# Chunk states by a scan that reads the sums in PSUM, and longer groups of small products on TensorE

## Chip, cores and metric

The kernel runs on one core of one Trainium2 chip. The metric is the device time of one execution in microseconds (us). TensorE (PE) multiplies matrices into PSUM, VectorE (DVE), ScalarE (ACT) and GpSimd (POOL) do the elementwise work, and SyncE (SP) issues every DMA, all on one queue.

## What is computed

Three stages run one after the other over 4 batches of 768 tokens: a gated linear attention with 8 heads of 48, a mixing block with a squared ReLU and a sigmoid gate, and a low-rank token mixing with a two-layer ReLU network.

```python
for t in range(S):                                   # attention, S = 768, D = 48
    state = alpha[:, :, t, :, None] * state + einsum('bhd,bhe->bhde', k[:, :, t], v[:, :, t])
    y[:, :, t] = einsum('bhd,bhde->bhe', q[:, :, t], state)
...
xk = mu_k * x + (1 - mu_k) * x_prev                  # first block; xr likewise with mu_r
k = maximum(xk @ w_k, 0);  v = k * k @ w_v;  r = sigmoid(xr @ w_r);  x = r * v
...
u = x + (x.T @ U @ V).T                              # second block
out = u + maximum(u @ w_ch1, 0) @ w_ch2
```

## The kernel before

**Tiling.** The tokens are cut into 8 half batches ("blocks") of 384 tokens. A block has two attention *units* of four heads, and a unit has two *phases* (`ph`) of two heads, one on partitions 0 to 47 (`EV`), the other on 64 to 111 (`OD`). There are 16 units. Even blocks are the first half of a batch, odd blocks the second; `unit(u)` gives that as `half`. A block's tokens are three chunks of 128 (`NC`, `CH`).

**Attention of a unit.** `prep` (line 700) makes, for each phase, running products of alpha with two DVE scans (`G` backwards, `Fp` forwards), the chunk factors `fc`, the scaled keys `KB` and the scaled queries `QG`. `scores` (722) multiplies keys by queries: three chunks for each of two heads, six products of 48x128 by 48x128, the heads in banks 6 and 7, then a DVE mask into `SC`. `keys_by_token` (733) transposes the three chunks of keys on PE into bank 5 and copies them (`KI`). `states` (742) makes the sums of keys times values, 12 small products (48 columns) in bank 5, and from them the states at the chunks' starts: ACT spreads the factors (`FX`) and copies the sums out of PSUM (`KV`, line 754), in a second half the carried state is scaled by ACT (four pieces) and added by DVE (two), DVE scans (multiply, then add), and two DVE products with the factors write the states `ST`. `outputs` (770) adds values times scores and states times queries, products with 128 columns in banks 6 and 7, and ACT copies the result into `x`; six small DMAs then spread a quarter of its rows over three tiles.

**Dense part.** `moe1` (897) and `moe2` (991) are long runs of products with 384 columns, three for each float32 pair (high and low parts). All eight blocks of `moe1`, with the attention of the following blocks woven in, come before all of `moe2`.

**Order.** Nothing is ordered by hand. `Plan` records every operation with a price in ns and a due time; `schedule` (186) lists them engine by engine, 11 times over with priorities drawn from the last pass, and keeps the order with the earliest planned end. On PE a switch between large products and small ones (`SHORT`: scores 165, outputs 107, states 60) has a price, so after a small product the next small one that is ready goes first if its priority is within `BATCH` of the best large one (line 242). Where the plan sees PE idle it puts a *fill* product (tile `warm`, line 395) of 56 ns, which writes nothing that is read. `dma` (361) prices a load by its words.

**Storage.** Keys, queries and alphas of a phase go to one of three tiles `T`. Converted rows of the second block's result leave through `x2_ring`, two slots; a third row tile waits until the DMA of the first has left its slot. Each fp32 product counts as two records in the trace; the large ones are fp32r and count as one.

Of the kernel before, what the change touches and what calls it, by code (L numbers as in the profile page):

```python
# [19 lines left out]
P = 128  # L20
# [23 lines left out]
    mix0_k=468, wk0=-238, wk1=-283, wk2=-17, wk3=45, wk4=60, wkk=7, wv=-12, r0=5, wr=37, early=31, x2=25, u=48, w1=227,  # L44
# [8 lines left out]
BATCH = 3000.0  # L53
# [26 lines left out]
class Plan:  # L80
# [265 lines left out]
    def scan(self, out, d0, d1):  # L346
        self.add(
            "DVE", 66.0 + 2.085 * out.free_size(), [out], [d0, d1],
            lambda: self.nc.vector.tensor_tensor_scan(  # L349
                out=out, data0=d0, data1=d1, initial=0.0, op0=ALU.mult, op1=ALU.add  # L350
            ), True,
        )
# [7 lines left out]
    def dma(self, out, in_, out_key=None, in_key=None, cost=650.0):  # L360
        words = 1
        for d in out.shape:
            words *= d
        self.add(
            "SP", max(cost, words / 90.0), [out if out_key is None else out_key], [in_ if in_key is None else in_key],
# [36 lines left out]
def fast_path(nc, plan, arena, rounded, shared, banks, qka, v, mus, w_k, w_r, w_v, U, V, w_1, w_2, out, x2d, ok_i):  # L402
# [45 lines left out]
    fc = new(NPH, NC)  # L448
# [10 lines left out]
    raw_at = [words(arena, 2 * TB) for _ in range(4)]  # L459
    raw_n = [0]  # L460
# [30 lines left out]
    FX, R = (att(2, D, NC) for _ in range(2))  # L491
    ST = [att(2, 2, NC, D) for _ in range(2)]
    KV = new(2, D, NC)
    carry = new(2, 2, D)
    G, Fp, bt = (att(TB) for _ in range(3))
    aC = new(NC)
# [57 lines left out]
    plan.dve(400, [bt], [], lambda: nc.vector.memset(bt, 0.0))  # L554

# [12 lines left out]
    plan.pool(130, [FX[:, :, :, 0]], [], lambda: nc.gpsimd.memset(FX[:, :, :, 0], 0.0))  # L568
    for t in banks[5:8]:
        plan.dve(600, [t[32:64]], [], lambda t=t: nc.vector.memset(t[32:64], 0.0))  # L570
# [104 lines left out]
    def tile_of(ph):  # L675
        return T[{2: 0, 3: 1, 0: 2, 1: 0}[ph] if ph < 4 else ph % 3]

    def load_qka(ph, parts=((0, KD),), rows=D, to=None):
# [4 lines left out]
        for a, z in parts:  # L683
            for hh in range(2):
                src = qka[b, h0 + hh, half, 0, a, 0]
                plan.dma(
                    t[64 * hh : 64 * hh + rows, a * TB : z * TB],
                    bass.AP(src.tensor, src.offset, [[KD * TB, rows], [1, (z - a) * TB]]), in_key="in", cost=475.0,
# [7 lines left out]
    def check_pair(ph, t):  # L696
        there = junk[:, 0 : t.free_size()].rearrange("p (c t) -> p c t", c=t.shape[1])
        plan.act(there, t, AF.Relu, scale=-1.0, bias=ALPHA_MIN, accum_out=low[:, ph : ph + 1])

    def prep(ph, due, engs):  # L700

        qt, kt, at = q_k_a(tile_of(ph))
        g0, f, a0 = G[:, 0:TB:CH], fc[:, ph, :], firsts[:, ph, :]
# [4 lines left out]
        first = at[:, 0:TB:CH]  # L708
        plan.act(a0, first, AF.Copy)
        plan.act(first, ends[:, 0:NC], AF.Copy)  # L710
# [3 lines left out]
        plan.pool(163, [f], [a0, g0], lambda: nc.gpsimd.tensor_tensor(out=f, in0=a0, in1=g0, op=ALU.mult))  # L714
        plan.at = due + 6
        plan.scan(Fp, at[:, 0:TB], bt)
        plan.at = due + 14
        plan.tt(KB[ph % 2], kt, G, ALU.mult, engs[0])
        plan.at = due + 17
        plan.tt(QG[ph % 4], qt, Fp, ALU.mult, engs[1])  # L720
# [13 lines left out]
    def keys_by_token(ph, due):  # L734
        plan.at = due
        kt, kb = sub(kk_b, NC, 112), KB[ph % 2]
        for c in range(NC):
            plan.transpose(kt[:, c, :], kb[BOTH, c * CH : (c + 1) * CH], ident[BOTH, BOTH])
        for h, r in enumerate((EV, OD)):
            plan.act(KI[ph % 2][:, h], kt[:, :, r], AF.Copy)  # L740
# [653 lines left out]
```

## Time and profile before

| | us |
|---|---|
| median of 3 runs | 724.15 (722.25 to 725.62) |
| the profiled execution, its own time | 724.62 |
| its span, first to last instruction | 722.9 |
| PE busy | 705.5 (98%) |
| DVE busy | 508.5 (70%) |
| ACT busy | 354.5 (49%) |
| fill products on PE | 581 |

The span has three parts. Up to about 127 us (the start) the attention of the first blocks is made, weights are loaded and converted, and large products begin; fill products stand there up to 73 us. From 127 to 450 us `moe1` runs with attention woven in. From 450 us on there are only `moe2` and its conversions. In a timeline row the length of merged products reaches to the modelled end of the last one, which overlaps the next row; how long a group holds PE is read from its start to the start of the next row.

### The profile page before, as it was taken

The page shows a single profiled execution, that of the slowest core. Times are in us where ns is not written, and L with a number is a line of the kernel's source. Part 1 is how long each engine was busy: PE and PEld are TensorE (multiplying, and loading weights), DVE is VectorE, ACT ScalarE, POOL GpSimd, SP SyncE. Part 2 cuts the span into 40 slices and gives each one's busy share as a digit, 9 for nine tenths or more (in the row PEclk, how much of TensorE's full clock was granted, in tenths as well). Part 3 has the DMA queues.
Part 4 walks back from the last instruction along what each step waited for, and adds up shares of the span by engine and source line. Part 5 has one row for each costly group of instructions (what it writes and reads, how often), then busy time and mean ns, then how long its engine had stood idle before and what let it go on. Part 6 is the DMA issues. An engine that isn't in the chain of part 4 may idle for free.

```text
span 722.9 us, 13907 instructions
## 1 busy us (share of the span) xinstructions
PE 705.5 (98%) x5319; PEld 675.4 (93%) x5319; DVE 508.5 (70%) x1173; ACT 354.5 (49%) x901; POOL 75.8 (10%) x131
## 2 busy tenths in 40 slices
PE   7999999999999999999999999999999999999995
PEld 7798889899999999999999999999999999999995
DVE  6898987897776567773699999575665657474611
ACT  2588656976767557677797672212121112111210
POOL 2021101442130311311002100000000000000000
PEclk9999989999999999999999999999999999999998
DMA  8835733434333222313253240102020202020001
GB/s 222 200 102 157 186 84 102 108 94 109 85 98 75 63 62 60 98 51 99 65 153 110 66 143 16 51 0 66 1 67 1 65 1 67 1 66 2 34 1 37
DMA packets 29484, 55.46 MB, mean 77 GB/s; under 512 B 5344, under 2 KB 20064, under 8 KB 29408
## 3 DMA queue, kind: packets, MB, share of 16 engines
q1 hardware_dynamic: 29408, 54.48, 27.3%
q8 instruction: 43, 0.70, 0.4%
q14 instruction: 33, 0.27, 0.1%
HBM read 43.85 MB, written 9.44 MB: 74 GB/s over the span
## 4 chain that ended last, share of the span: by engine, by line
PE 74%; DVE 6%; ACT 4%; DMA 3%; issue 1%; SPq 1%; DVEq 0%; ACTq 0%
PE bank L305 73%; DMA arena<-in_qka_dram 3%; ACT arena L320 2%; DVE arena L137 2%; DVE arena L982 2%; DVE rounded L137 1%; PE bank L310 1%; SPq L366 1%; ACT rounded L320 1%; DVE shared L137 1%; ACT shared L320 1%; DMA out_dram<-arena 0%; ACT bank L320 0%; DVE shared L349 0%; DVEq L137 0%
## 5 line engine op out<-in xcount | busy, mean ns | idle before, releaser
L305 PE MATMUL bank<-rounded 128*128 128x384 f32 x2232 | 424.3, 339 | 2.9 <-ACT rounded L320 1.2
L305 PEld LDWEIGHTS bank<-rounded 128*128 128x128 f32 x2232 | 383.7, 186 | 13.2 <-ACT arena L320 2.2
L305 PE MATMUL bank<-rounded,shared 128*128 128x384 f32 x864 | 164.9, 335 | 0.8 <-DVE rounded L137 0.5
L320 ACT ACTIVATE rounded<-bank 128x384 fp32r<-128x384 f32 x160 | 78.3, 489 | 175.4 <-PE bank L305 174.3
L305 PEld LDWEIGHTS bank<-rounded,shared 128*128 128x128 f32 x864 | 150.9, 188 | 1.7 <-DVE rounded L137 1.0
L320 ACT ACTIVATE arena<-arena 128x384 f32<-128x384 f32 (+6 forms) x234 | 103.2, 463 | 48.2 <-DMA arena<-in_qka_dram 29.4
L137 DVE SCALAR_TENSOR_TENSOR rounded<-bank,rounded 128x384 fp32r<-128x384 f32 x96 | 53.4, 556 | 91.4 <-ACT rounded L320 90.3
L982 DVE STREAM_TRANSPOSE arena<-arena 32x96 f32<-32x96 f32 x384 | 103.8, 270 | 5.7
L305 PE MATMUL bank<-shared 128*48 128x128 f32 (+3 forms) x1472 | 100.3, 266 | 3.4 <-DMA shared<-in_v_dram 1.2
L305 PEld LDWEIGHTS bank<-shared 128*48 128x48 f32 (+2 forms) x1472 | 86.6, 142 | 17.8 <-issue 6.2
L320 ACT ACTIVATE rounded<-arena 128x384 fp32r<-128x384 f32 (+2 forms) x137 | 70.4, 522 | 63.6 <-DVE arena L982 49.4
L137 DVE SCALAR_TENSOR_TENSOR arena<-arena 128x384 int32<-128x384 int32 (+2 forms) x140 | 79.9, 590 | 8.9 <-ACT arena L320 8.3
L320 ACT ACTIVATE bank<-bank 128x384 f32<-128x384 f32 x128 | 61.6, 482 | 23.4 <-PE bank L305 22.7
L137 DVE TENSOR_TENSOR rounded<-arena,rounded 128x384 fp32r<-128x384 f32 (+1 forms) x108 | 60.5, 570 | 11.4 <-ACT rounded L320 10.9
L137 DVE TENSOR_TENSOR arena<-bank,arena 128x384 f32<-128x384 f32 (+1 forms) x76 | 41.5, 552 | 25.0 <-PE bank L305 9.9
L137 DVE TENSOR_TENSOR rounded<-bank,rounded 128x384 fp32r<-128x384 f32 x64 | 35.4, 552 | 30.6 <-ACT rounded L320 28.9
L320 ACT ACTIVATE arena<-bank 112x384 f32<-112x384 f32 (+3 forms) x76 | 37.3, 504 | 35.2 <-PE bank L305 33.3
L137 DVE TENSOR_TENSOR shared<-bank,arena 128x384 f32<-128x384 f32 x64 | 33.9, 547 | 24.5 <-PE bank L305 23.0
L137 POOL TENSOR_TENSOR rounded<-arena,rounded 128x384 fp32r<-128x384 f32 (+1 forms) x25 | 27.7, 1116 | 110.5 <-ACT rounded L320 110.4
L395 PE MATMUL bank<-warm 128*128 128x128 bf16 x581 | 37.4, 224 | 1.1 <-DVE arena L543 1.1
L395 PEld LDWEIGHTS <-warm 128*128 128x128 bf16 x581 | 34.5, 101 | 3.1 <-issue 1.5
L349 DVE TENSOR_TENSOR_SCAN shared<-arena 128x384 f32<-128x384 f32 x32 | 31.0, 967 | 4.4 <-ACT arena L320 4.3
(47 smaller groups left out, 258.3 us busy)
## 6 DMA issues: line engine op xcount, KB each, us to landing
arena<-in_qka_dram SPq DMA_DIRECT2D x56, 216.0 KB, 3.7
arena<-in_w_dram SPq DMA_DIRECT2D x24, 384.0 KB, 3.5
shared<-in_v_dram SPq DMA_DIRECT2D x32, 144.0 KB, 3.0
x2d<-arena SPq DMA_DIRECT2D x24, 192.0 KB, 2.2
arena<-x2d SPq DMA_DIRECT2D x8, 576.0 KB, 4.1
out_dram<-arena SPq DMA_DIRECT2D x24, 192.0 KB, 1.9
arena<-in_w_v_dram SPq DMA_DIRECT2D x8, 384.0 KB, 3.2
arena<-in_qka_dram SPq DMA_DIRECT2D x24, 72.0 KB, 2.0
```

What stands on the lines that cost most here:

```text
L137: fn(**args)
L305: "PE", cost, [out], [lhsT, rhs], lambda out, lhsT, rhs: fn(out, lhsT=lhsT, rhs=rhs, start=start, stop=stop),
L310: self.add("PE", cost, [out], [in_, ident], lambda: self.nc.tensor.transpose(out, in_, ident))
L320: self.add("ACT", cost, outs, [in_] + extra, lambda out, in_: fn(out, in_, func, **kw), out=out, in_=in_)
L349: lambda: self.nc.vector.tensor_tensor_scan(out=out, data0=d0, data1=d1, initial=0.0, op0=ALU.mult, op1=ALU.add), True,
L366: lambda: self.nc.sync.dma_start(out, in_),
L395: lambda i: nc.tensor.matmul(banks[SPARE[i]][:, 384:512], lhsT=warm, rhs=warm, start=True, stop=True), FILL_UNTIL, ROUNDS
L982: plan.dve(284, [to], [src], lambda to=to, src=src: nc.vector.transpose(out=to, in_=src))
```

## The change

- `states`: the products write each sum with a stride of four words into bank 5 (one slot more than before, `NC + 1`). The scan reads the sums straight from PSUM, adds first and then multiplies by the factor, so that its results are the states; ACT copies them into `ST`. The DVE products, the ACT copy of the sums and, in a second half, the scaling and adding of the carried state are gone: the carried state is copied by ACT into the spare slot of bank 5. In a second half the last chunk's state is not needed, and its keys are not transposed and its sums not made.
- `prep`: the lower bound on the decay is taken inside the scan `G` (its second operation is a maximum), in place of a POOL operation ahead of the reciprocal.
- Planner: `BATCH` 3000 to 15000, a load is priced at words/56 in place of words/90, and the due times of the `w_k` loads are others; their pieces are 1, 1, 3, 1, 1, 1 in place of 1, 2, 3, 1, 1 columns of 128.
- A fourth tile `T[3]` lies over two buffers of weights, so that all four phases of the first block have their own tile. In the first block the spreading DMAs follow the unit that is made first.
- `moe2`: the three result tiles go to `rs`, three slots, in place of `x2_ring`.
- Several operations take 112 partitions in place of 128.

```diff
-    mix0_k=468, wk0=-238, wk1=-283, wk2=-17, wk3=45, wk4=60, wkk=7, ...
+    mix0_k=468, wk0=-238, wk1=-230, wk2=-220, wk3=38, wk4=45, wk5=60, wkk=7, ...
-BATCH = 3000.0
+BATCH = 15000.0
...
-    def scan(self, out, d0, d1):
+    def scan(self, out, d0, d1, op0=ALU.mult, op1=ALU.add):
...
-            "SP", max(cost, words / 90.0), ...
+            "SP", max(cost, words / 56.0), ...
...
+    T.append(view(arena, raw_at[2], (KD * TB + 1,)))
...
-        nc.vector.memset(ends, 0.0)
+        nc.vector.memset(ends, DECAY_MIN)
...
-        return T[{2: 0, 3: 1, 0: 2, 1: 0}[ph] if ph < 4 else ph % 3]
+        return T[{2: 0, 3: 1, 0: 2, 1: 3}[ph] if ph < 4 else ph % 3]
...
-        plan.scan(G[:, ::-1], at[:, 1 : TB + 1][:, ::-1], ends[:, ::-1])
-        plan.pool(160, [aC], [g0], lambda: nc.gpsimd.tensor_scalar_max(out=aC, in0=g0, scalar1=DECAY_MIN))
-        plan.dve(110, [bt], [aC], lambda: nc.vector.reciprocal(bt[:, 0:TB:CH], aC))
+        plan.scan(g[:, ::-1], at[:, 1 : TB + 1][:, ::-1], ends[BOTH, ::-1], op1=ALU.max)
+        plan.dve(90, [bt], [g], lambda: nc.vector.reciprocal(bt[BOTH, 0:TB:CH], g[:, 0:TB:CH]))
...
-        for c in range(NC):
+        m = NC - unit(ph // 2)[1]
+        for c in range(m):
             plan.transpose(kt[:, c, :], kb[BOTH, c * CH : (c + 1) * CH], ident[BOTH, BOTH])
...
-        kv, vs, st = sub(kk_b, 2, NC, D), VS[u % 2], ST[u % 2]
+        kv, vs, st = sub(kk_b, 2, D, NC + 1), VS[u % 2], ST[u % 2]
+        last = carry[BOTH, u % 2]
+        if half:
+            plan.act(kv[BOTH, :, :, 0], last, AF.Copy)
         for j in range(2):
-            for c in range(NC):
+            for c in range(NC - half):
                 for h, r in enumerate((EV, OD)):
-                    plan.mm(kv[r, j, c, :], KI[j][:, h, c, :], vs[:, h, c, j, :], True, True, plan.S48)
-        plan.act(FX[BOTH, :, :, 1:], f[:, :, 1:].unsqueeze(2).to_broadcast([112, 2, D, NC - 1]), AF.Copy)
-        plan.act(KV[BOTH].rearrange("p j d c -> p j c d"), kv[BOTH], AF.Copy)
-        if half:
-            for j in range(2):
-                for h, r in enumerate((EV, OD)):
-                    plan.act(st[r, h, j, 0, :], carry[r, u % 2, j], AF.Copy, scale=fc[r, 2 * u + j, 0:1])
-            for h, r in enumerate((EV, OD)):
-                plan.tt(KV[r, :, :, 0], KV[r, :, :, 0], st[r, h, :, 0, :], ALU.add)
-        plan.scan(*(t[BOTH].rearrange("p j d c -> p (j d c)") for t in (R, FX, KV)))
-        for h, r in enumerate((EV, OD)):
-            plan.tt(st[r, h, :, 1:, :], R[...], fc[...], ALU.mult)
+                    plan.mm(kv[r, j, :, half + c], KI[j][:, h, c, :], vs[:, h, c, j, :], True, True, plan.S48)
+        plan.act(FX[BOTH], f.unsqueeze(2).to_broadcast([112, 2, D, NC + 1]), AF.Copy)
+        plan.scan(*(t[BOTH].rearrange("p j d c -> p (j d c)") for t in (R, kv, FX)), ALU.add, ALU.mult)
+        for h, r in enumerate((EV, OD)):
+            plan.act(st[r, h, :, 1 - half :, :], R[...], AF.Copy)
...
-            outputs(u, due + 30, i == 1)
+            outputs(u, due + 30, i == 0, i == 1)
...
-            o = x2_ring()
+            o = rs[:, t, :]
```

On PE, in the second block of `moe1` (large products in banks 3 and 4, scores in banks 6 and 7, state sums in bank 5), before:

```order
L305 MATMUL bank5_78<-shared_72 48x48 x5
L305 MATMUL bank4_77<-rounded_71 128x384 x2
L305 MATMUL bank6_79<-shared_72 128x128 x3
L305 MATMUL bank7_80<-shared_72 128x128 x3
L305 MATMUL bank5_78<-shared_72 48x48 x7
L305 MATMUL bank3_76<-rounded_71 128x384 x8
L305 MATMUL bank6_79<-shared_72 128x128 x3
L305 MATMUL bank7_80<-shared_72 128x128 x3
```

The same place after:

```order
L305 MATMUL bank5_78<-shared_72 48x48 x8
L305 MATMUL bank4_77<-rounded_71 128x384 x4
L305 MATMUL bank6_79<-shared_72 128x128
L305 MATMUL bank7_80<-shared_72 128x128
L305 MATMUL bank6_79<-shared_72 128x128
L305 MATMUL bank7_80<-shared_72 128x128
L305 MATMUL bank6_79<-shared_72 128x128
L305 MATMUL bank7_80<-shared_72 128x128
L305 MATMUL bank3_76<-rounded_71 128x384 x6
```

The unit's state sums, 12 before in two pieces, are 8 in one piece, and the scores of the two heads alternate between their banks in place of three and three.

On SP in the start, from the last values of the first block on, before (`arena<-arena` with 16 rows are the spreading DMAs):

```order
L366 DMA shared_72<-in_v_dram 128x288
L366 DMA arena_70<-in_w_k_dram 128x3x256
L366 DMA arena_70<-in_w_k_dram 128x3x512
L366 DMA arena_70<-in_mu_dram 128x6
L366 DMA arena_70<-in_qka_dram 48x1152 x2
L366 DMA arena_70<-in_w_k_dram 128x3x768
L366 DMA arena_70<-arena_70 16x384 x3
```

and after:

```order
L366 DMA shared_72<-in_v_dram 128x288 x2
L366 DMA arena_70<-in_w_k_dram 128x3x256 x2
L366 DMA arena_70<-in_mu_dram 128x6
L366 DMA arena_70<-arena_70 16x384 x4
L366 DMA arena_70<-in_w_k_dram 128x3x768
L366 DMA arena_70<-arena_70 16x384 x2
L366 DMA arena_70<-in_w_k_dram 128x3x256 x2
L366 DMA arena_70<-in_qka_dram 48x1152 x2
```

The largest load of `w_k` (768 columns of words) stood ahead of the spreading DMAs and now stands behind four of them; the next block's keys stood ahead of it and now follow all of `w_k` but one piece.

## Rows read from the trace of the kernel before

**Rows 1.** Windows: us, each engine's busy time and instructions, granted clock, DMA share, GB/s.
```profile
core 0: us, PE busy (x) PEld busy (x) DVE busy (x) ACT busy (x) POOL busy (x), PEclk, DMA share, GB/s
0.00:74.00 74.00, 67.21 (x890) 61.63 (x891) 60.20 (x127) 46.74 (x123) 11.09 (x31) 1.00 0.64 171
74.00:127.00 53.00, 52.09 (x480) 45.41 (x478) 45.49 (x87) 31.59 (x92) 4.94 (x12) 0.94 0.49 121
99.45:103.30 3.85, 3.85 (x23) 2.89 (x22) 2.73 (x6) 2.02 (x6) 0.00 (x0) 1.00 0.38 102
103.30:110.20 6.90, 6.90 (x48) 6.23 (x49) 4.71 (x9) 2.01 (x6) 0.38 (x2) 0.51 0.37 86
127.00:450.00 323.00, 320.88 (x2426) 303.59 (x2422) 248.48 (x525) 225.43 (x585) 59.79 (x88) 1.00 0.31 86
450.00:715.60 265.60, 265.32 (x1529) 264.75 (x1529) 153.73 (x436) 50.77 (x102) 0.00 (x0) 1.00 0.10 31
```

**Rows 2.** Timeline of PE at 711 us and DVE's last add: start, length, what.
```profile
714.95 0.69 PE L305 MATMUL bank<-shared,rounded 128*128 128x384 f32 x3
...
716.72 0.56 DVE L137 TENSOR_TENSOR arena<-bank,arena 128x384 f32<-128x384 f32 x1 [1.19 <-DMA out_dram<-arena]
```

**Rows 3.** Timeline of PE, 86 us: one unit's 24 records of state sums.
```profile
86.11 0.74 PE L305 MATMUL bank<-shared 128*48 128x48 f32 x24
86.78 0.44 PE L305 MATMUL bank<-rounded 128*128 128x384 f32 x1
```

**Rows 4.** Timeline of PE, 162 us: a group of large products between small ones.
```profile
162.97 1.75 PE L305 MATMUL bank<-shared 48*128 48x128 f32 x26
164.65 1.66 PE L305 MATMUL bank<-rounded 128*128 128x384 f32 x8
166.24 1.26 PE L305 MATMUL bank<-shared 48*128 48x128 f32 x12
167.43 1.85 PE L305 MATMUL bank<-rounded 128*128 128x384 f32 x9
```

**Rows 5.** Timeline of PE, 223 us: alternating scores, then three transposes.
```profile
223.38 0.94 PE L305 MATMUL bank<-shared 48*128 48x128 f32 x12
224.25 1.14 PE L305 MATMUL bank<-rounded 128*128 128x384 f32 x5
225.23 0.45 PE L310 MATMUL bank<-arena,shared 112*128 112x112 f32 x3
225.45 1.11 PE L305 MATMUL bank<-rounded 128*128 128x384 f32 x5
```

**Rows 6.** Timeline of PE: output products, a group of 16 records and one of 40.
```profile
118.38 1.08 PE L305 MATMUL bank<-shared 128*48 128x128 f32 x16
119.39 0.79 PE L305 MATMUL bank<-rounded 128*128 128x384 f32 x3
...
217.24 2.40 PE L305 MATMUL bank<-shared 128*48 128x128 f32 x40
219.57 3.88 PE L305 MATMUL bank<-rounded 128*64 128x384 f32 x21
```

**Rows 7.** Timeline of PE, 42 us: the longest stretch of fill products.
```profile
42.69 10.67 PE L395 MATMUL bank<-warm 128*128 128x128 bf16 x188
53.20 0.46 PE L310 MATMUL bank<-arena,shared 112*128 112x112 f32 x3
```

**Rows 8.** Groups of DVE by form, whole span: count, busy us, mean ns.
```profile
...
L137 DVE TENSOR_TENSOR shared<-shared,arena 48x192 f32<-48x192 f32 x32 | 13.1, 409 | 0.4
L349 DVE TENSOR_TENSOR_SCAN shared<-shared,arena 112x288 f32<-112x288 f32 x16 | 11.9, 747 | 1.1 <-ACT arena L320 1.1
L137 DVE TENSOR_TENSOR arena<-arena,shared 48x96 f32<-48x96 f32 x16 | 4.5, 279 | 0.3
```

**Rows 9.** Timeline of SP in the start: the largest load of `w_k`, the first spreading DMAs.
```profile
16.15 0.56 SPq L366 DMA_DIRECT2D arena<-in_w_k_dram  x1
24.85 1.87 SPq L366 DMA_DIRECT2D arena<-arena  x3
```

More of the change, by code (lines that the diff above doesn't have):

```diff
@@ L349, in scan @@
             lambda: self.nc.vector.tensor_tensor_scan(
-                out=out, data0=d0, data1=d1, initial=0.0, op0=ALU.mult, op1=ALU.add
-            ), True,
+                out=out, data0=d0, data1=d1, initial=0.0, op0=op0, op1=op1
+            ), self.in_sbuf(d0, d1),
         )
@@ L364, in dma @@
         self.add(
-            "SP", max(cost, words / 90.0), [out if out_key is None else out_key], [in_ if in_key is None else in_key],
+            "SP", max(cost, words / 56.0), [out if out_key is None else out_key], [in_ if in_key is None else in_key],
             lambda: self.nc.sync.dma_start(out, in_),
@@ L447, in fast_path @@
     low = new(NPH)
-    fc = new(NPH, NC)
+    fc = new(NPH, NC + 2)
     firsts = new(NPH, NC)
@@ L490, in fast_path @@
     VS = [att(2, NC, 2, D) for _ in range(2)]
-    FX, R = (att(2, D, NC) for _ in range(2))
+    FX, R = (att(2, D, NC + 1) for _ in range(2))
     ST = [att(2, 2, NC, D) for _ in range(2)]
[L493 to L496, printed above, removed]
+    carry = att(2, 2, D)
+    G, Fp = (att(TB) for _ in range(2))
+    bt = new(TB)
     w1h, w1l = (view(shared, i * KD * DF2, (KD, DF2), F32R) for i in range(2))
@@ L554, in fast_path, with make_fc @@
     plan.dve(400, [bt], [], lambda: nc.vector.memset(bt, 0.0))
+    plan.pool(60, [low], [], lambda: nc.gpsimd.memset(low, 0.0))
+    def make_fc():
+        nc.gpsimd.memset(fc, 0.0)
+        nc.gpsimd.memset(fc.rearrange("p (b h n) c -> p b h n c", b=B, h=2)[:, :, 0, :, NC], 1.0)
+    plan.pool(200, [fc], [], make_fc)
     def make_tri():
@@ L567, in fast_path @@
         plan.pool(600, [t], [], lambda t=t: nc.gpsimd.memset(t, 0.0))
[L568 to L570 removed]
+    for t in (banks[5], banks[6][32:64], banks[7][32:64]):
+        plan.dve(600, [t], [], lambda t=t: nc.vector.memset(t, 0.0))
     def next_raw():
@@ L696, in check_pair @@
     def check_pair(ph, t):
-        there = junk[:, 0 : t.free_size()].rearrange("p (c t) -> p c t", c=t.shape[1])
-        plan.act(there, t, AF.Relu, scale=-1.0, bias=ALPHA_MIN, accum_out=low[:, ph : ph + 1])
+        there = junk[BOTH, 0 : t.free_size()].rearrange("p (c t) -> p c t", c=t.shape[1])
+        plan.act(there, t, AF.Relu, scale=-1.0, bias=ALPHA_MIN, accum_out=low[BOTH, ph : ph + 1])
     def prep(ph, due, engs):
-        qt, kt, at = q_k_a(tile_of(ph))
-        g0, f, a0 = G[:, 0:TB:CH], fc[:, ph, :], firsts[:, ph, :]
+        qt, kt, at = (t[BOTH] for t in q_k_a(tile_of(ph)))
+        g, fp, f, a0, first = G[BOTH], Fp[BOTH], fc[BOTH, ph, 0:NC], firsts[BOTH, ph, :], at[:, 0:TB:CH]
         if ph >= CHECK_LATER:
@@ L790, in outputs @@
         for j in range(2):
-            plan.act(x[BOTH, p0 + j, 1:], two_b[j][BOTH, 0:TB], AF.Copy)
+            for r in (EV, OD) if apart else (BOTH,):
+                plan.act(x[r, p0 + j, 1:], two_b[j][r, 0:TB], AF.Copy)
         if spread:
```

66 lines of the change are left out of this document (31 added, 35 removed).

## Prediction

> **What bounds the kernel now.** I read the windows first, one line for each part of the span, because the shares of the whole span average over parts with different limits [rows 1]. From 127 to 450 us PE is busy 320.88 of 323.00 us (99%), while DVE has 248.48 and ACT 225.43; from 450 to 715.60 us PE is busy 265.32 of 265.60. So over four fifths of the kernel PE is the bound, and an edit is worth there what PE no longer does. Work taken from DVE or ACT is worth nothing there. In the second stretch 1529 large products fill 265.32 us, 0.174 us each. Before 74 us PE looks busy too (67.21 of 74.00), but much of that is fill: 188 fill products stand in one row, 42.69 to 53.20 us, 0.056 us each [rows 7], and there are 581 of them, all before 73 us, some 32 us together. In that part DVE is the busiest engine that does real work (60.20 of 74.00), and PE waits for what DVE, ACT and the loads bring. The third thing to see is a stretch at the lower clock: from 103.30 to 110.20 us PE is busy without a gap, and the granted clock is 0.51, which is the 1.2 GHz level; the 3.85 us ahead of it hold only 23 instructions, one head's six score records in turn with one or two large products. At half speed half of its 6.90 us is lost, about 3.4 us. Last, the tail: the last large products end about 715.64, and the third add starts at 716.72, after an idle time of 1.19 us that a DMA out of the two-slot ring ended [rows 2].
>
> **The profiled execution against the median.** The sum is made in the profiled execution's own time, 724.62 us, whose span is 722.9. It lies 0.47 above the median of the runs, 724.15, and I take that off at the end.
>
> **State sums.** A unit made 24 records (12 products) and now makes 24 in a first half, 16 in a second. What a record costs: 24 in one piece hold PE from 86.11 to 86.78, 0.67 us [rows 3]. A group of 26, from 162.97 to 164.65, holds 12 score records and 14 of state sums, 1.68 us; the 12 scores alone take 1.19 (166.24 to 167.43) [rows 4], so 14 records took 0.49. The slope is (0.67 - 0.49) / 10 = 0.018 us for a record, and 0.49 - 14 x 0.018 = 0.24 us remains for each group. These records are cheap, and the separate pieces are not. In the order as it is built, from the 252nd large product on (136.6 us before; from there on PE does not starve) there are 240 records in 18 pieces before and 192 in 12 after: 48 x 0.018 + 6 x 0.24 = 2.3 us less. It is all on the path, since PE is the bound there. The pitch of a record is taken as unchanged although its target is now strided; that is the third rival below.
>
> **Transposes.** Three take 0.22 us, 225.23 to 225.45 [rows 5], 0.073 each. From the same point there are 54 before and 44 after: 0.7 us.
>
> **Longer groups.** A set of scores written as three of one head, then three of the other takes the 1.19 us above; one that alternates between the two banks takes 0.87, 223.38 to 224.25 [rows 5], so 0.32 less. From the 252nd large product on the straight sets go from 11 to 2: nine of them, 2.9 us. I count the three mixed sets of the new order with the alternating ones. Output products: 16 records hold PE 1.01 us and 40 hold it 2.35 [rows 6]; for 8 and 20 products that is 0.11 for a product and 0.12 for a group. The products stay, the groups go from 14 to 10: 0.5 us. A group of large products between small ones has an entry price: 8 took 164.65 to 166.24, 1.59 us [rows 4], against 8 x 0.174 = 1.39, so 0.20. There is only one such switch less (22 to 21): 0.2 us. `BATCH` is worth little for switches; nearly all of its gain is in how the scores alternate and in whole pieces of state sums.
>
> From 136.6 us on: 2.3 + 0.7 + 2.9 + 0.5 + 0.2 = 6.6 us.
>
> **Tail.** With three slots the third add waits for nothing but its product, so it starts at about 715.64 in place of 716.72: 1.1 us less. What is late next is the product itself. The last DMA moves with the add.
>
> **DVE and ACT.** A unit loses two multiplies of 0.409 us, its scan goes from 288 to 384 elements, and in a second half two adds of 0.279 go too [rows 8]. I estimate the new scan at 0.747 x 384 / 288 = 1.0 us. Reading PSUM has no row for a scan; the bounds are that pitch and twice it, 2.0. So a first half loses 0.82 - 0.25 = 0.57 us, a second half 1.13, and units 0 to 5, which lie in the first 127 us, some 4.6 us together. ACT gets two copies into `ST` for the four scalings and the copy of the sums. From 127 us on none of it counts, since DVE has 323 - 248 = 75 us to spare there and ACT 98; if a scan of 2.0 us comes out, ten units add 10 us to a DVE with 75 free. The new chain holds bank 5 until the scan has read it; it used to be free after an ACT copy. What is queued behind that on PE is the next unit's transposes and sums, and large products cover it.
>
> **The start.** The gain is at least the fills that the new order no longer sees a need for, 581 - 538 = 43, 43 x 0.056 = 2.4 us, if they are the shortest view of it, and at most all of DVE's 4.6. The stretch at the lower clock is a second term: the longer groups leave fewer alternations ahead of it, but scores still stand between few large products there, so it lies between 0 and 3.4 us less. I take 2.4 and half of the 3.4, 1.7, together 4.1. The bounds for the start are +3 (next paragraph), and -8.0 (4.6 + 3.4).
>
> **Loads.** SP is one queue. The largest load of `w_k` (1152 KB) was issued at 16.15 us, the first spreading DMAs at 24.85, when the wait for the first outputs ended [rows 9]. Now four spreads stand ahead of the load, so it and the rest of `w_k` and the keys of the next block wait with them: 8.7 us later unless the unit made first is done sooner. The cover: between its issue and the products that need the whole of `w_k` PE has all of those fills, and the DMA engines are at 0.64 before 74 us [rows 1], so 1152 KB at that window's 171 GB/s is 6.7 us in a queue with room. I cost it at nothing; with the cover gone it is part of 8.7 us, as the conversions behind it spread, and I take 3 as its bound.
>
> **Sum.** 724.62 - 6.6 - 1.1 - 4.1 = 712.8, and 0.5 less against the median: **712.3 us**.
>
> **Rivals.** First, what the start gains is lost again, or the long groups wait for their last operand. For it: the late `w_k`, and a group that is closed up with small products of a later phase gives less cover to each. Against it: large products stand ready from 127 us on, and PE's idle time there is 2.1 us in all. A start at 0 gives 712.3 + 4.1 = 716.4; at +3 it is 719.4; with 0.5 us of wait for each of the 12 late groups of state sums on top of a start at 0, 722. Chance 0.20, a quarter of that above 720.5.
>
> Second, the start follows DVE wholly and the low clock goes: 712.3 + 4.1 - 8.0 = 708.4, and with the 2.1 us of PE's idle time gone too, 706.3. For it: DVE is the busiest real worker before 74 us. A deeper cut, to 705, needs a part of the remaining fills as well. Chance 0.15.
>
> Third, the one that ends slower: PE writes the state sums four words apart, and the record's pitch is set by the writing. Every product in this trace writes contiguous words, so no row shows it. The bounds are the contiguous pitch, 0.018 (nothing), and a large product's 0.174. At an output record's 0.11 / 2 = 0.055, 320 records in all cost 320 x (0.055 - 0.018) = 11.8 us and the result is 724; at 0.174, 50 us and 762. Below 0.018 there is no reason to go, since the order of words doesn't shorten the columns that PE streams. It decides for slower (above 727.8) from (727.8 - 712.3) / 320 = 0.048 us more, a pitch of 0.067. I take the nearest row, the contiguous records of the same shape, because 48 columns in 0.018 us is the same pitch that the large product shows (384 in 0.174 is 0.022 for 48), which leaves no sign that writing is what bounds. Chance 0.07. The Trainium skill, page "PSUM — Partial Sum Buffer", section "Specifications (TRN2)", speaks for this rival: it gives 8-byte cachelines and says that "any non-contiguous AP slows matmuls significantly". It gives no factor, and no run so far shows it; by that rule the sum would be on the rival's side, at whatever pitch it brings.
>
> That the change doesn't do what it says can be put aside: the order shows fewer records, fewer pieces and the alternating scores.
>
> **Chances and range.** About 0.5% (3.6 us) is what a measurement of this kernel can tell from no change, so faster is below 720.5 and slower above 727.8. The forecast with its own spread (708 to 716) has 0.55, the first rival 0.20, the second 0.15, the third 0.07, and 0.03 is left for a loss of middle size. Faster: 0.55 + 0.15 + 0.15 = 0.85. Same: the 0.05 of the first rival and the 0.03, 0.08. Slower 0.07. The range takes the forecast, most of the second and most of the first: 705 to 719.5.
>
> **What would show it.** State sums: a piece of 16 or 24 records at 0.018 us for each and a group's price; a pitch of 0.05 or more makes the third rival right. Scores: 12 records in 0.87 us nearly everywhere. Tail: the third add with no wait for a DMA, and the end 1.1 us nearer to the last product. Start: the last fill before 73 us, by 2 to 5 us, and a window near 105 us with a clock above 0.51. DVE: a scan from PSUM of about 1.0 us. Loads: the `w_k` load's issue later than 16.15, and no weight conversion that PE waits for behind it. PE must still be busy 99% from 127 us on; if its idle time there is above 5 us, the long groups wait and the first rival holds. The forecast is wrong if the stretch behind 127 us gives less than 4 us, whatever the start does.

## The result, and the profile after

The changed kernel takes **700.96 us** (median of 4 runs, 699.97 to 701.26) against 723.21 for the kernel before in the same comparison (722.25 to 725.62): ratio 0.9685, 95% interval 0.9657 to 0.9714. The forecast of faster was right. The forecast of size was not: 22 us went away where 12 were foretold, and 700.96 lies below the range.

Windows of the changed kernel, columns as in [rows 1]:

```profile
0.00:74.00 74.00, 72.76 (x950) 68.23 (x951) 66.08 (x135) 54.36 (x142) 6.75 (x29) 1.00 0.71 190
74.00:127.00 53.00, 52.88 (x444) 47.57 (x445) 47.19 (x88) 39.66 (x108) 9.86 (x14) 1.00 0.52 125
127.00:450.00 323.00, 321.25 (x2410) 306.56 (x2409) 235.72 (x500) 219.07 (x553) 48.47 (x59) 1.00 0.30 84
450.00:692.20 242.20, 242.20 (x1397) 241.64 (x1395) 141.27 (x403) 46.26 (x93) 0.00 (x0) 1.00 0.09 28
```

Against [rows 1], the first line has changed most: PE is busy 72.76 of 74 us in place of 67.21, DVE 66.08 in place of 60.20, ACT 54.36 in place of 46.74. All three engines do more in the same stretch, so what has gone there is waiting. The granted clock is 1.00 up to 450 us.

To see where the 23.4 us went that PE ends earlier, I take the times at which the same large product starts in both traces (there are 3168, one record each):

| large product | before, us | after, us | difference |
|---|---|---|---|
| first | 41.01 | 30.36 | -10.7 |
| after 72 | 71.81 | 62.28 | -9.5 |
| the 252nd itself | 136.61 | 121.82 | -14.8 |
| after 252 | 139.08 | 121.99 | -17.1 |
| after 1101 (attention ends) | 353.93 | 331.45 | -22.5 |
| last | 715.29 | 691.90 | -23.4 |

The two orders have done the same work at the start of the 252nd product, from which the prediction counted: 156 score records, the state sums of six units and 256 output records. Right behind it the kernel before makes 12 score and 24 state sum records, which the changed kernel makes later. Timeline of PE in the kernel before:

```profile
137.40 1.75 PE L305 MATMUL bank<-shared 128*48 128x48 f32 x36 [0.46 <-ACT shared L320]
139.08 2.20 PE L305 MATMUL bank<-rounded 128*128 128x384 f32 x11
```

So at equal work 14.8 us lie in the start, where the prediction had 4.1, and 8.6 behind it, where it had 6.6. The windows and the table below reach to the next large product (139.08 and 121.99 us), which puts 2.3 us more into the start of the kernel before.

**State sums with strided targets.** Timeline of PE in the changed kernel: 12 alternating score records with 16 state sum records behind them, 12 alternating score records alone, and in the first block 12 straight ones with 24 of state sums:

```profile
20.11 1.94 PE L305 MATMUL bank<-shared 48*128 48x128 f32 x36
21.98 0.40 PE L395 MATMUL bank<-warm 128*128 128x128 bf16 x4
...
60.92 1.43 PE L305 MATMUL bank<-shared 48*128 48x128 f32 x28
62.28 3.05 PE L305 MATMUL bank<-rounded 128*128 128x384 f32 x16
65.26 0.94 PE L305 MATMUL bank<-shared 48*128 48x128 f32 x12
66.13 0.41 PE L310 MATMUL bank<-arena,shared 112*128 112x112 f32 x2
```

The 28 records hold PE 62.28 - 60.92 = 1.36 us and the 12 scores alone 66.13 - 65.26 = 0.87, so 16 strided records take 0.49 us. The price of the prediction gives 0.24 + 16 x 0.018 = 0.53. The 36 hold it 1.87, less 1.19 for straight scores [rows 4] 0.68 for 24 strided records, against 0.67 for 24 contiguous ones [rows 3]. A target four words apart costs nothing here. The third rival falls. For these products the trace doesn't agree with what the prediction quoted for it from the Trainium skill (page "PSUM — Partial Sum Buffer", section "Specifications (TRN2)").

**Scan.** Groups of DVE by form in the changed kernel:

```profile
L349 DVE TENSOR_TENSOR_SCAN shared<-arena 112x384 f32<-112x384 f32 x64 | 62.4, 986 | 3.6 <-ACT arena L320 1.6 <-POOL shared L137 1.5 <-issue 0.2
L349 DVE TENSOR_TENSOR_SCAN shared<-bank,shared 112x384 f32<-112x384 f32 x16 | 15.2, 949 | 7.0 <-PE bank L305 7.0
```

The scan that reads PSUM takes 0.949 us, no longer than one that reads SBUF (0.986); the estimate was 1.0.

**Tail.** PE's last large products and DVE's last add in the changed kernel:

```profile
691.56 0.69 PE L305 MATMUL bank<-shared,rounded 128*128 128x384 f32 x3
692.28 0.56 DVE L137 TENSOR_TENSOR arena<-bank,arena 128x384 f32<-128x384 f32 x1 [0.31 <-PE bank L305]
```

The add starts 0.03 us after the products' end (691.56 + 0.69); before it was 1.08 [rows 2]. Not all of that reached the end: the span ends 6.8 us after the last products, before 7.3. SP issues the last three output DMAs here, before and after:

```profile
713.13 4.51 SPq L366 DMA_DIRECT2D out_dram<-arena  x3
```

```profile
691.13 2.83 SPq L366 DMA_DIRECT2D out_dram<-arena  x3
```

Before, they end 0.36 us after the add (717.64 against 717.28), now 1.12 us after it (693.96 against 692.84), so part of the wait has moved to SP. In e8, which has the same order on all engines, the span ends 6.3 us after the last products.

**The start.** Two windows that reach from 0 to the start of the large product behind the 252nd, the first of the kernel before, the second of the changed one:

```profile
0.00:139.08 139.08, 130.93 (x1468) 117.24 (x1468) 115.69 (x230) 88.88 (x246) 23.09 (x54) 0.98 0.58 150
```

```profile
0.00:121.99 121.99, 120.75 (x1366) 111.23 (x1367) 108.98 (x214) 89.60 (x238) 16.41 (x42) 1.00 0.64 166
```

DVE's busy time falls from 115.69 to 108.98, by 6.7 us (by 5.0 up to the 252nd itself, close to the prediction's 4.6). The rest, 10.4 us, is DVE's idle time, 23.4 before and 13.0 after. The prediction had bounded the start by DVE's busy time, as if there were no such idle time. A view that the prediction did not read points at where it came from, ACT's waits. Up to the same two points, for the loads of queries, keys and alphas (us in total, times, longest), before and after:

```profile
ACT arena L320 <- DMA arena<-in_qka_dram: 19.5, 12, 3.6
```

```profile
ACT arena L320 <- DMA arena<-in_qka_dram: 8.2, 6, 3.0
```

### The profile page after: what moved, and what is told of

It reads as the page before. It is cut to its first block, busy times and chain, and to the rows that moved or that the text cites. A ratio compares the mean times of both kernels' runs of the same rounds, so it can differ in the third digit from the quotient of the medians.

```text
span 699.1 us, 13588 instructions
## 1 busy us (share of the span) xinstructions
PE 689.1 (99%) x5196; PEld 664.0 (95%) x5196; DVE 490.8 (70%) x1125; ACT 359.3 (51%) x895; POOL 65.1 (9%) x102
## 4 chain that ended last, share of the span: by engine, by line
PE 83%; DVE 8%; ACT 4%; DMA 2%; issue 1%; POOL 0%; SPq 0%; DVEq 0%; ACTq 0%; POOLq 0%
PE bank L305 78%; PE bank L395 4%; DVE rounded L137 3%; DVE arena L137 2%; DVE arena L987 2%; ACT arena L320 1%; DMA arena<-in_qka_dram 1%; ACT rounded L320 1%; PE bank L310 1%; ACT shared L320 1%; ACT bank L320 1%; DVE shared L349 1%; DVE shared L137 0%; DMA arena<-in_V_dram 0%; POOL shared L137 0%
## 5 line engine op out<-in xcount | busy, mean ns | idle before, releaser
L305 PE MATMUL bank<-rounded 128*128 128x384 f32 x2232 | 419.1, 338 | 0.5 <-DVE rounded L137 0.2
L320 ACT ACTIVATE arena<-arena 128x384 f32<-128x384 f32 (+6 forms) x234 | 101.6, 463 | 20.5 <-DMA arena<-in_qka_dram 14.9
L320 ACT ACTIVATE rounded<-arena 128x384 fp32r<-128x384 f32 (+3 forms) x137 | 70.2, 522 | 63.9 <-DVE arena L987 48.4
L305 PEld LDWEIGHTS bank<-shared 128*48 128x48 f32 (+2 forms) x1408 | 78.7, 140 | 13.2 <-issue 6.2
L305 PE MATMUL bank<-shared 128*48 128x128 f32 (+3 forms) x1408 | 90.7, 264 | 0.0
L137 DVE SCALAR_TENSOR_TENSOR arena<-arena 128x384 int32<-128x384 int32 (+2 forms) x140 | 78.9, 583 | 11.5 <-ACT arena L320 10.9
L349 DVE TENSOR_TENSOR_SCAN shared<-arena 112x384 f32<-112x384 f32 x64 | 62.4, 986 | 3.6 <-ACT arena L320 1.6
L320 ACT ACTIVATE arena<-bank 112x384 f32<-112x384 f32 (+3 forms) x62 | 29.6, 490 | 23.7 <-PE bank L305 23.0
L395 PE MATMUL bank<-warm 128*128 128x128 bf16 x538 | 35.3, 228 | 1.1 <-DVE arena L543 1.1
L395 PEld LDWEIGHTS <-warm 128*128 128x128 bf16 x538 | 33.0, 103 | 2.4 <-DVE arena L543 1.1
(46 smaller groups left out, 209.5 us busy)
```

Of the source, the lines that this page charges most:

```text
L137: fn(**args)
L305: "PE", cost, [out], [lhsT, rhs], lambda out, lhsT, rhs: fn(out, lhsT=lhsT, rhs=rhs, start=start, stop=stop),
L320: self.add("ACT", cost, outs, [in_] + extra, lambda out, in_: fn(out, in_, func, **kw), out=out, in_=in_)
L349: lambda: self.nc.vector.tensor_tensor_scan(out=out, data0=d0, data1=d1, initial=0.0, op0=op0, op1=op1), self.in_sbuf(d0, d1),
L395: lambda i: nc.tensor.matmul(banks[SPARE[i]][:, 384:512], lhsT=warm, rhs=warm, start=True, stop=True), FILL_UNTIL, ROUNDS
```

## The experiments

All times are medians (e16 is one execution); the kernel before lay between 722.4 and 724.4 us in these comparisons. "Start" is the time up to the large product behind the 252nd, "load waits" is the row just shown, up to that point.

| run | us | ratio to before (95%) | start, us | DVE busy in it | load waits, us |
|---|---|---|---|---|---|
| before | 723.2 | | 139.1 | 115.7 | 19.5 |
| before, second profile (e16) | 720.3 | | 134.4 | 115.6 | 18.3 |
| changed kernel | 701.0 | 0.9685 (0.9657 to 0.9714) | 122.0 | 109.0 | 8.2 |
| e1 arithmetic alone | 712.9 | 0.9859 (0.9803 to 0.9915) | 129.9 | 111.8 | 15.4 |
| e2 planner and loads alone | 712.7 | 0.9845 (0.9793 to 0.9897) | 130.1 | 116.1 | 10.7 |
| e3 old states | 709.0 | 0.9787 (0.9736 to 0.9839) | 128.3 | 115.6 | 6.5 |
| e4 old prep | 700.8 | 0.9681 (0.9630 to 0.9732) | 123.9 | 111.2 | 6.9 |
| e5 BATCH 3000 | 702.8 | 0.9727 (0.9679 to 0.9775) | 125.2 | 110.0 | 8.6 |
| e6 words/90 | 709.4 | 0.9818 (0.9770 to 0.9866) | 126.1 | 108.1 | 19.3 |
| e7 old w_k pieces | 703.9 | 0.9734 (0.9685 to 0.9783) | 124.6 | 109.7 | 9.7 |
| e8 three tiles, old spreads | 700.3 | 0.9687 (0.9640 to 0.9734) | 123.2 | 109.0 | 9.4 |
| e9 price alone, in before | 714.6 | 0.9876 (0.9839 to 0.9913) | 131.8 | 117.0 | 9.0 |
| e10 words/72 | 710.1 | 0.9807 (0.9767 to 0.9846) | 134.1 | 112.0 | 16.0 |
| e11 more DVE work, outside the chain | 699.7 | 0.9692 (0.9644 to 0.9740) | 123.2 | 113.2 | 10.3 |
| e12 last chunk made again | 702.8 | 0.9732 (0.9687 to 0.9776) | 122.6 | 112.1 | 4.0 |
| e13 words/64 | 704.3 | 0.9738 (0.9680 to 0.9796) | 125.0 | 109.6 | 11.8 |
| e14 words/48 | 703.4 | 0.9731 (0.9674 to 0.9788) | 124.6 | 110.9 | 2.3 |
| e15 scan twice, inside the chain | 705.2 | 0.9753 (0.9695 to 0.9810) | 128.5 | 113.7 | 10.1 |
| e17 arithmetic and price | 700.1 | 0.9691 (0.9654 to 0.9727) | 121.4 | 108.6 | 6.5 |
| e18 arithmetic, price, slots | 699.3 | 0.9653 (0.9620 to 0.9687) | 121.7 | 108.8 | 6.6 |

### Arithmetic or planner

e1 is the changed kernel with these lines, and the due times of the `w_k` loads, as before; e2 is the kernel before with all of them as in the change, but `outputs(u, due + 30, i == 0)`:

```diff
 BATCH = 3000.0
 self.add("SP", max(cost, words / 90.0), ...
 return T[{2: 0, 3: 1, 0: 2, 1: 0}[ph] if ph < 4 else ph % 3]
 outputs(u, due + 30, i == 1, i == 1)
 ((P, raw_at[0]), (2 * P, raw_at[1]), (3 * P, rs_at), (P, raw_at[3]), (P, raw_at[0]))
 o = x2_ring()
```

> The changed kernel with all planner and load parts as before (BATCH 3000, words/90, the old w_k pieces and due times, three tiles T, the spreading DMAs at their old place, two result slots); only the states by the scan over PSUM and the maximum inside prep's scan are new. Theory A (the start was bound by the chain of DVE work in each unit, so the arithmetic gave the start its 17 us): 703 to 708 us, the first large product at about 30 us as in the changed kernel, and some 3 to 5 us of group prices lost behind 127 us. Theory P (the loads' order and the planner's numbers gave it): 713 to 719, the first large product near 40 us.

> The kernel before with all planner and load parts of the change (BATCH 15000, words/56, new w_k pieces and due times, fourth tile, spreads, three result slots), and the old states and prep. Theory A: 716 to 721 us, 592 fill products and the first large product at 37 us or later. Theory P: 704 to 710, the first large product near 31 us. In both the last add waits for no DMA.

In e2 the copy of the unit made second also covers the rows that the spreading DMAs have filled, since that copy was not split. Its result is therefore wrong, and it is shown for its time alone; its work is the same but for two copies.

Both theories fall. Each half gives 11 to 12 us, 712.9 and 712.7, and together they give the whole. In the start both stand near 130 us.

### The two halves of the arithmetic

```diff
-        plan.scan(... (R, kv, FX)), ALU.add, ALU.mult)
+        (states of the kernel before, lines 754 to 766)
```

> The changed kernel with the states as before (sums copied by ACT, scan of 288, two multiplies, scaling and adding the carried state, all 12 sums and three transposes in a second half); prep's scan stays new. Theory A: 594 fill products, 708 to 713 us, of it about 3 us behind the 252nd large product and the rest in the start. Theory P: 703 to 706, all of it behind the 252nd large product.

```diff
-        plan.scan(g[:, ::-1], ..., ends[BOTH, ::-1], op1=ALU.max)
+        plan.scan(g[:, ::-1], ..., ends[BOTH, ::-1], op1=ALU.add)
+        plan.pool(160, [aC], [g], lambda: nc.gpsimd.tensor_scalar_max(...))
```

> The changed kernel with prep's lower bound again as a POOL maximum between the scan and the reciprocal. Theory A, in the form that the chain's latency counts and not only DVE's busy time: 556 fill products, 2 to 5 us more (703 to 706), all in the start, though DVE does the same work. If only DVE's busy time counts: 700 to 702.

Undoing the states costs 8.0 us, more than half of it in the start. Undoing prep costs nothing (700.8), so Theory A missed in the form that it had for e4: its start is longer by 1.9, but it has made 12 score and 16 state sum records more by then, and its attention ends at 331.1 us where the changed kernel's ends at 331.5.

### The planner's numbers one by one

```diff
-BATCH = 15000.0
+BATCH = 3000.0
```

> The changed kernel with BATCH 3000. If BATCH acts as the prediction had it (scores alternate, whole pieces of state sums): 3 to 5 us more behind the 252nd large product (704 to 706) and little in the start. If it also sets the start's stalls: more than 706.

```diff
-            "SP", max(cost, words / 56.0), ...
+            "SP", max(cost, words / 90.0), ...
```

> The changed kernel with a load priced at words/90. Theory L (DVE's idle time in the start is time that ACT waits for loads of keys, queries and alphas; the true price lets the plan issue them so that they are there): 705 to 711, ACT's waits for these loads up to 127 us near 15 us in place of 8.2, and DVE idle up to the 252nd large product near 20 us in place of 13.0. Rival: the price moves nothing, 700 to 702.

```diff
-        ((P, raw_at[0]), (P, raw_at[1]), (3 * P, rs_at), (P, raw_at[2]), (P, raw_at[3]), (P, raw_at[0]))
+        ((P, raw_at[0]), (2 * P, raw_at[1]), (3 * P, rs_at), (P, raw_at[3]), (P, raw_at[0]))
...
```

> The changed kernel with the pieces and due times of the w_k loads as before. Theory W (the w_k load ahead of the next keys and of the spreads cost the start its stalls): 704 to 709, 584 fill products, the first large product at 34 us. Rival: 700 to 702.

```diff
-        return T[{2: 0, 3: 1, 0: 2, 1: 3}[ph] if ph < 4 else ph % 3]
+        return T[{2: 0, 3: 1, 0: 2, 1: 0}[ph] if ph < 4 else ph % 3]
-            outputs(u, due + 30, i == 0, i == 1)
+            outputs(u, due + 30, i == 1, i == 1)
```

> The changed kernel with phase 1 in the first tile again and the spreading DMAs where they were; the order of all engines stays the same. If the fourth tile spares a wait for the tile: 1 to 4 us more, with a wait for a load of phase 1 before 12 us. If the tile is free by then anyway: 700 to 702.

One of them carries the time: the price of a load, 8.5 us (709.4). With words/90 ACT waits for the loads as long as in the kernel before, in e6:

```profile
ACT arena L320 <- DMA arena<-in_qka_dram: 19.3, 10, 3.7
```

Theory L had DVE idle 20 us there; it is 126.1 - 108.1 = 18.0. Half of the 8.5 us lies in the start (4.1), the other half between the 252nd and the 1101st large product (213.7 us against 209.5), where large products wait (beyond 0.1735 us each they take 11.5 us there, against 7.6). `BATCH` is worth 1.9 us, below what e5 expected, the pieces of `w_k` 2.9 (703.9, between the two ranges of e7), the fourth tile and the spreads nothing.

### The price by itself, and other prices

> The kernel before with one number changed: a load is priced at words/56 in place of words/90. Theory L (the price of the loads is what took DVE's and ACT's waits out of the start): 713 to 718 us, ACT's waits for the loads of keys, queries and alphas up to the 252nd large product at 8 to 12 us in place of 19.5, DVE busy there unchanged at 116. Rival (the price helps only together with the new pieces of w_k, the fourth tile and BATCH): 720 to 725.

One number in the kernel before gives 8.7 us (714.6), as Theory L expected, with the load waits at 9.0 and DVE's busy time little changed (117.0). In e9:

```profile
ACT arena L320 <- DMA arena<-in_qka_dram: 9.0, 7, 2.5
```

A part of the 8.7 us is the lower clock, which many executions of the kernel before have (see the part on the clock below).

What a load takes is seen in a window of the kernel before (the last number is GB/s):

```profile
0.00:41.00 41.00, 35.51 (x516) 31.97 (x516) 30.43 (x65) 19.33 (x58) 6.04 (x27) 1.00 0.80 205
```

205 GB/s are 51 words of 4 bytes per ns. A price of words/90 plans with 360 GB/s, words/56 with 224. The 205 is a mean over 41 us in which the DMA engines are busy 0.80. With words/90 the planner believed that data was there which was still on its way. Three more prices:

```diff
-            "SP", max(cost, words / 56.0), ...
+            "SP", max(cost, words / 72.0), ...   (e10; 64.0 in e13, 48.0 in e14)
```

> The changed kernel with the price at words/72, half way. Theory L: between the two, 703 to 707, with ACT's waits for those loads between 8 and 19 us. Rival (the planner's order jumps at random between prices, and 56 happened to be a good one): anywhere from 700 to 712, with no relation to the waits.

> The changed kernel with a load priced at words/64. If the price acts by its value: 700 to 704, start (to the 252nd large product) 122 to 126 us. If the orders jump: outside of that, as the 134 us of words/72 was outside of the 122 to 126 of 56 and 90.

> The changed kernel with a load priced at words/48, just slower than the 205 GB/s (51 words per ns) that the first 41 us of the kernel before show. If the price acts by its value, with its best near the measured rate: 700 to 704. If being careful costs time (577 fill products in place of 538, planned waits that need not be): 703 to 708. If the orders jump: anywhere up to 712.

The load waits follow the price without a break: 19.3, 16.0, 11.8, 8.2 and 2.3 us at 90, 72, 64, 56 and 48. In e14:

```profile
ACT arena L320 <- DMA arena<-in_qka_dram: 2.3, 1, 2.3
```

The time follows less strictly: 709.4, 710.1, 704.3, 701.0, 703.4. It is lowest at 56, next to the measured 51, and the one price that is more careful than the rate, 48, takes waits away and loses elsewhere. e10 missed what Theory L expected: one stop of PE and the lower clock behind it, described in the last section, are part of it. e13 lies just above its range; its fastest execution, with a mean granted clock of 0.998, took 702.8 us, and the others, with 0.995 to 0.996, 703.7 to 705.4. That the orders also jump from price to price by a few us is not excluded.

### DVE's busy time or the chain

```diff
+        plan.tt(junk[:, 0:TB], ends, ends, ALU.mult)
         plan.at = due + 6
         plan.scan(fp, at[:, 0:TB], bt[BOTH])
```

> The changed kernel with one more DVE product of 128x384 (ends times ends into the junk tile, which nothing reads) in each prep, 12 of them in units 0 to 5: 12 x 0.55 = 6.6 us of DVE work in the start that no chain waits for. If DVE's busy time bounds the start: 705 to 707.5, all of it before the 252nd large product. If it fits into DVE's idle 13.0 us there: 700 to 702.

```diff
         plan.scan(*(...(R, kv, FX)), ALU.add, ALU.mult)
+        plan.scan(*(...(R, kv, FX)), ALU.add, ALU.mult)
```

> The changed kernel with the scan of the states done twice, the second time with the same result, so that 0.95 us more stand inside each unit's chain between its sums and its outputs; units 0 to 5 get 5.7 us of DVE work in the start, about what e11 added outside of the chain. Theory C (the chain's length counts in the start, DVE's busy time doesn't): 2 to 6 us more, 702.5 to 706.5, and 590 fill products. If neither counts: 700 to 702.

Windows up to the large product behind the 252nd, of e11 and of e15:

```profile
0.00:123.21 123.21, 120.92 (x1384) 110.44 (x1385) 113.22 (x222) 88.22 (x234) 15.24 (x40) 1.00 0.65 164
```

```profile
0.00:128.50 128.50, 125.25 (x1418) 113.38 (x1419) 113.70 (x221) 90.31 (x237) 17.77 (x40) 1.00 0.60 158
```

DVE is busy 113.2 and 113.7 us there, 4.2 and 4.7 more than in the changed kernel. Outside of the chain that costs nothing (699.7; start +1.2). Inside of it, between a unit's sums and its outputs, it costs 4.2 us (705.2; start +6.5). So DVE's busy time doesn't bound the start, and time between a unit's sums and its outputs counts. That does not hold for each part of the chain: e4 put a POOL operation back into `prep` and cost nothing. Nor is the 4.2 us sure to be the chain alone, since the planner makes a new order for every added operation (590 fill products in e15, 556 in e11, 538 in the changed kernel).

### Last chunk

```diff
-        m = NC - unit(ph // 2)[1]
+        m = NC
-            for c in range(NC - half):
+            for c in range(NC):
...
```

> The changed kernel, but a second half again transposes its last chunk of keys and makes the four sums for it (64 records and 16 transposes more in all). By the prediction's prices, behind the 252nd large product: 48 x 0.018 + 10 x 0.073 = 1.6 us, so 702 to 703.5; if small records cost what a row of the trace shows as pitch only when waiting, up to 706.

702.8, 1.9 us more against 1.6 worked out from the prices of the prediction. All of it lies behind the 252nd large product (211.3 us to the 1101st against 209.5). That the two numbers are so near is in part luck. By kind of record, counted as in the part on why, the state sums cost 1.4, the transposes 0.9 and the scores 0.8 more, and the large products give 1.3 back.

### Arithmetic and price together

e17 is e1 with words/56; e18 is e17 with `o = rs[:, t, :]`.

> The kernel of e1 (only the new states and prep) with one number more: a load priced at words/56. If these two carry the gain and the rest is worth what e5, e7 and e8 showed one by one plus the tail (1.9 + 2.9 + 0 + 1.1): 703 to 708. If the other parts matter more together than one by one: 709 to 713, hardly below e1.

> The kernel of e17 with the three result slots of the change and nothing else. If the last add's wait for the DMA (1.17 us in e17) is the tail: 699.0, 1.0 to 1.2 us below e17. If the last DMA then lands later by as much: 700. Below the changed kernel (700.96) in either case.

e17 missed both of its ranges, to the low side. These two edits are the change: 700.1, the same as with everything else. So `BATCH`, the pieces of `w_k`, the fourth tile and the spreads give nothing that a measurement can tell, although undoing the first two one at a time cost 1.9 and 2.9. Where the largest load of `w_k` stands doesn't decide either. SP in e17, where it is the last of three that go ahead of the spreads, and in the changed kernel, where it follows four of them:

```profile
11.98 1.94 SPq L366 DMA_DIRECT2D arena<-in_w_k_dram  x3
18.32 4.75 SPq L366 DMA_DIRECT2D arena<-arena  x6
```

```profile
18.73 2.49 SPq L366 DMA_DIRECT2D arena<-arena  x4
21.26 0.60 SPq L366 DMA_DIRECT2D arena<-in_w_k_dram  x1
```

In both the spreads start 6 us earlier than before [rows 9], because the unit that they wait for is done earlier. The three slots on top give 699.3, and the last add shows why. DVE's last add in e17 and in e18:

```profile
692.20 0.56 DVE L137 TENSOR_TENSOR arena<-bank,arena 128x384 f32<-128x384 f32 x1 [1.17 <-DMA out_dram<-arena]
```

```profile
692.01 0.56 DVE L137 TENSOR_TENSOR arena<-bank,arena 128x384 f32<-128x384 f32 x1 [0.31 <-PE bank L305]
```

e18, with `BATCH`, the pieces of `w_k`, the fourth tile and the spreads as in the kernel before, is below both kernels in its median; against the changed kernel's 700.96 its 0.2% are less than a measurement can tell from no change.

## Why the prediction was right or wrong, point by point

**The stretch that PE bounds: right in its terms.** From the 252nd large product to the 1101st, adding up for each record the time to the next record's start, by kind: state sums 8.5 to 6.0 us (2.5 less; the prediction had 2.3), transposes 4.5 to 3.7 (0.8; 0.7), scores 22.2 to 19.2 (3.0; 2.9), outputs 26.3 to 25.6 (0.7; 0.5), large products beyond 0.1735 each 8.3 to 7.6 (0.7, of it 0.46 the wait ahead of the 36 records shown further up; 0.2). That is 7.7 less against 6.6, and 0.9 more comes behind the 1101st, where the prediction had nothing. Two small readings of it are off and change nothing: the 40 output records hold PE 2.33 us by [rows 6], not 2.35, and DVE's terms add up to 4.5, not 4.6. Counting the mixed sets of scores with the alternating ones was luck: a set cut in two takes 0.86 for each half, 1.7 in all, but the kernel before has two such sets as well.

**But not in what it was put down to.** The scores' 3 us were credited to `BATCH`. With BATCH 3000 (e5) they take 18.3 us for 216 records, while with BATCH 15000 and the old states they take 21.8 (e2) and 22.0 (e3). In the order as it is built, straight sets behind the 252nd large product are 2 in the changed kernel and in e5, 8 in e2, 9 in e3, and 11 in e12, where only the last chunk is made again. The alternation comes with the dropped chunk, by way of the planner. e12 takes only 0.8 us more for its scores than the changed kernel (20.0 against 19.2), since none of its sets is cut in two.

**Tail: right in its cause.** The wait is gone, 1.08 to 0.03. From the last products to the end of the span, 0.4 us of it was seen in the changed kernel's profile, and 0.9 from e17 to e18 (7.2 to 6.3 us), where the three slots are the only edit; the prediction had 1.1.

**The start: wrong, by 10.7 us** (14.8 against 4.1). Three steps failed.

1. "At most all of DVE's 4.6." DVE was taken for the bound because it was the busiest engine with real work, 60.20 of 74 us [rows 1]. The busy time that went was sized about right (5.0). Its idle time was not asked after, and 9.8 us of that went too (5.3 against a second profile of the kernel before, e16). e11 shows that its busy time isn't the bound, and e15 that time between a unit's sums and its outputs counts.
2. The price of a load had no term in the sum. The prediction costs only the load that the new order moves. The price is worth 8.7 us alone (e9) and 8.5 when undone (e6); ACT's waits for loads go from 19.5 to 9.0 us when it alone is changed, and from 8.2 to 19.3 when it is undone.
3. "The gain is at least the fills that the new order no longer sees a need for." Words/90 has fewer fills than words/56 (517 against 538 in the order) and waits more, since a fill is placed where the plan, and not the chip, sees PE idle. Time in which PE is not busy was not counted, and the first line of [rows 1] showed 6.8 us of it, of which 5.6 went.

The cost of the later `w_k`, on the other hand, was rightly put at nothing: its issue moved from 16.15 to 21.26 us, and e17, which issues it ahead of the spreads, is as fast.

**The lower clock: right as a term.** The 3.4 us were in the profile of before, and half of them was in the sum. A second profile of the same kernel (e16) has no such stretch, and its large product behind the 252nd comes 4.66 us earlier with the same order (1.15 of it stands already at the first large product):

> The kernel before, unchanged, for a second profile. If the stretch at the lower clock belongs to its order: it comes again between 100 and 115 us, 3.4 us lost. If it comes by chance of one execution: none, or at another place, and the time near 720.

```profile
74.00:127.00 53.00, 52.24 (x500) 45.44 (x499) 48.26 (x93) 35.37 (x103) 9.05 (x17) 1.00 0.52 134
```

The granted clock is 1.00 where it was 0.94 [rows 1]. The executions on record tell how often it comes. Of 46 executions of the kernel before beside the experiments, 31 have a mean granted clock below 0.996 (median 724.0 us) and 15 have 0.996 to 0.998 (median 720.8). The four of the changed kernel have 0.997 to 0.998. So some 2 to 3 us of the 22 are the lower clock, near the 1.7 of the sum, and against the 15 the change is worth 19.8 us and the price alone 6.2.

Against the profile of e16 the start lost 12.4 us (10.2 at the 252nd itself), e1's 4.5, e9's 2.6, and that of both together (e17) 13.0. The two need each other: with the arithmetic alone ACT still waits 15.4 us for loads, with the price alone the chain has its old length. That each hides the other is my reading; no run follows it wait by wait.

**Rivals.** The second, a shorter start, came closest, 706.3 at its end; it went further by the load waits, which it did not have. The first and the third did not happen.

## What to carry to other kernels

In a stretch where no engine is full, the busiest engine's busy time need not be the bound: list the waits of every engine there, loads first, and ask which chain they lie on. A planner's price is part of the kernel: hold each against the rate that the trace shows (here 360 GB/s planned, 205 moved), because a price that was too low was paid here as waits that no fill covers. When an edit has many parts, run the two that carry it alone before crediting the rest.

## What the runs showed of the hardware

The lower clock comes by execution and by order: of two profiles of the kernel before one has it, while all four executions of e10 have a mean granted clock of 0.990 to 0.994 and all four of the changed kernel 0.997 to 0.998. Of the twenty profiles three have a stretch at the 1.2 GHz level inside the work: that of before, e10 and e13. In e10 PE had stood still just ahead of it. Two windows and PE's row there:

```profile
60.00:70.40 10.40, 6.22 (x51) 5.21 (x46) 9.09 (x18) 8.43 (x20) 0.36 (x1) 1.00 0.56 126
70.44:77.26 6.82, 6.20 (x25) 5.46 (x27) 5.01 (x11) 4.02 (x10) 0.36 (x1) 0.50 0.53 148
```

```profile
71.06 1.01 PE L305 MATMUL bank<-rounded 128*128 128x384 f32 x2 [3.75 <-ACT rounded L320]
```

PE was busy 6.22 of 10.40 us, waited 3.75 us for ACT, and the granted clock fell to 0.50, the 1.2 GHz level, for the next 6.82 us. In e13 PE had waited 1.59 us ahead of 3.41 us at that level. So there a stop was followed by a second cost; that the stop brought it about was not tested. In the profile of before the stretch followed small products between single large ones, with no stop.

Products with a target four words apart, and a scan that reads PSUM, cost the same as their plain forms, as the prediction had assumed (0.68 us for 24 records against 0.67; 0.949 us against 0.986).
